# Regrouping transposed x and the attention rows R by way of HBM, in six transfers a block where there were sixteen

## The chip, the cores and the metric

The kernel runs on one core of one Trainium2 chip. The metric is the device time of one execution in microseconds (us), as the median of several runs. Differences below about 0.3% (3.4 us) cannot be told from no change in this kernel.

A core has five engines with a queue each: PE (TensorE, matmuls; its weight loads are listed as PEld), DVE (VectorE), ACT (ScalarE), POOL (GpSimd) and SP (SyncE). SP computes nothing here: it issues nearly all DMA transfers, one after the other, in the order in which the program wrote them. An instruction that waits, on any engine, holds everything written behind it on that engine.

## What is computed

Two stages over x of shape (4, 12608, 128). The first is an attention by way of 32 inducing rows, used forth and back; the second is a channel mix with a shift by one token.

```python
h = mab(I, x)                  # 32 rows attend to all 12608 tokens of a batch
x = mab(x, h)                  # each token attends to the 32 rows of h
x_prev = shift(x, 1)           # the token before, 0 for the first
xk = mu_k * x + (1 - mu_k) * x_prev
xr = mu_r * x + (1 - mu_r) * x_prev
k = maximum(xk @ w_k, 0)       # 128 -> 1024
v = k * k @ w_v                # 1024 -> 128
out = sigmoid(xr @ w_r) * v
# mab(q, kv): softmax(q @ kv.T / sqrt(128)) @ kv
```

## The kernel before, in words

**The mix sets the rhythm.** The second attention's output is never formed. Its weights R (32 rows a token, held as rounded part and remainder) go straight into matmuls with W, which is h folded into the weights of the mix. Tokens of a batch are taken in 25 groups: 24 of 512 tokens and one of 320. A group takes four *units*, so there are 100 units a batch and 400 in all, emitted by the loop `for n in range(len(units) + LAG + 2)`. In unit n, PE first runs `up` of unit n (L809, L811: W times R into PSUM), then, in a group's second unit, `zgate` (L798, L799), then `down` of unit n - 4 (L840, six matmuls). DVE squeezes the result of `up` (L821, L823), ACT squares it (L826, L827), POOL takes a difference (L829). When a group is done, DVE multiplies by the gate (L845) and transposes the result (L856, in `store`), and for every second group SP issues four output transfers (L864) of 128 KB each.

**The attention is woven in by hand.** `at(n, f)` files a step f to be emitted at the end of unit n, after that unit's `down`; `soon(n, f)` files it right behind `up` of unit n. Steps of one n keep the order in which they were filed. In the loop the output transfers of a finished group stand ahead of the steps of the same unit: the store of group g falls into unit 4g + 9, for odd g of a batch in units 13, 21, 29 and so on, counted from the first unit of that batch.

A *block* is four groups (2048 tokens); a batch has six blocks and the short rest. With t the batch's first unit (4 in the first batch) and s = t + 12 j:

- `stage_a(b + 1, j, at, s)` treats block j of the *next* batch. `btr(c)`, for c = 0..3 at s - 1, s, s + 1, s + 3, transposes a quarter of the block in 32 x 32 squares on DVE (L344) into an `xs` tile of 128 x 512. Its four 32-row strips belong to four groups, and four transfers (L347) bring each to rows 32c..32c+31 of one group's transposed x (`xt`). So a block takes 16 transfers of 64 KB. The scores (L372: eight matmuls, all reading `xt`) are filed at s + 9, and the load of the following block (L193, 1 MB) at s + 5.
- `stage_b(b, j + 1, at, s + 1)` makes R of the next block of the *running* batch: scores (L616), softmax, then `high` (ACT, L656, the rounded part `ah`) at 7 and `low` (DVE, L660, the remainder `al`) at 9 units behind its start, and `spread(i)` for i = 0..3 at 10 + i. Each spread makes one group's R tile of 128 x 513: its column 0 is the last column of the group before (`halo`, L593, a transfer of 0.5 KB), and its four 32-row quarters are ah, al, ah, al of that group (L670, four transfers of 64 KB). The first unit that reads the block j + 1 of a batch is unit 16 (j + 1) of that batch. For the first of these blocks that is 16 units into the batch, against a first spread at unit 11 of it; later blocks have ever more time, since blocks are made every 12 units and used every 16. A `quick` variant, with fewer units between its steps, serves block 1 of the first batch and block 0 of the second.
- The first block of the first batch is made in the head (`start`), by transposes on PE and copies on ACT into R (`put`, L771 and L773), with three one-column copies on DVE for column 0 (L595). The copy for group 1 (`put1`) is filed behind `up` of unit 2, and the gate's weights (`wg`) and the scores of groups 2 and 3 (`sc2`) at the end of unit 1.

Of the kernel before, what the change touches and what calls it, by code (L numbers as in the profile page):

```python
# [19 lines left out]
def kernel(  # L20
# [11 lines left out]
    nc = tc.nc  # L32
# [21 lines left out]
    st = ctx.enter_context(tc.tile_pool(name="st", bufs=1))  # L54
    wp = ctx.enter_context(tc.tile_pool(name="wp", bufs=2))
    sm = ctx.enter_context(tc.tile_pool(name="sm", bufs=2))
    r_pool = ctx.enter_context(tc.tile_pool(name="r_pool", bufs=10))
    mp = ctx.enter_context(tc.tile_pool(name="mp", bufs=2))
    pa = ctx.enter_context(tc.tile_pool(name="pa", bufs=2, space=bass.MemoryType.PSUM))
    pv = ctx.enter_context(tc.tile_pool(name="pv", bufs=2, space=bass.MemoryType.PSUM))  # L60
    pb = ctx.enter_context(tc.tile_pool(name="pb", bufs=1, space=bass.MemoryType.PSUM))
# [26 lines left out]
    def load_weight(dst, src, n, raw):  # L88


        if src.dtype == F32:
            nc.sync.dma_start(out=dst, in_=src)
            return lambda: None
        raw = raw.bitcast(I32)[:, :2 * n]
        rv = raw
        if len(src.shape) == 3:
            rv = raw.rearrange("p (c d) -> p c d", c=src.shape[1])
        nc.sync.dma_start(out=rv, in_=src.bitcast(I32))

        def steps():  # L100
            v = nc.vector
            w2 = raw.rearrange("p (n h) -> p h n", h=2)
            lo, hi = w2[:, 0, :], w2[:, 1, :]
            o = next(turns)
            t = st.tile([P, G], I32, name=("s2", "ah")[o])[:, :n]
            q = st.tile([P, G], F32, name=("e1t", "aT")[o], bufs=1)[:, :n]
            m = st.tile([P, G], I32, name="xs", bufs=4)[:, :n]
            r = st.tile([P, G], I32, name="xs", bufs=4)[:, :n]
            qv, tv = q, t.bitcast(F32)
            if len(dst.shape) == 3:  # L110
                qv = qv.rearrange("p (c d) -> p c d", d=C)
                tv = tv.rearrange("p (c d) -> p c d", d=C)
            v.tensor_scalar(out=t, in0=hi, scalar1=20, scalar2=0x7FF,
                            op0=ALU.logical_shift_right, op1=ALU.bitwise_and)
            nc.scalar.activation(out=t, in_=t, func=AF.Relu, scale=-1.0, bias=bias[0])
            nc.scalar.activation(out=t, in_=t, func=AF.Relu, scale=-2.0 ** 23, bias=bias[1])
            v.tensor_scalar(out=m, in0=hi, scalar1=0xFFFFF, scalar2=0x100000,
                            op0=ALU.bitwise_and, op1=ALU.bitwise_or)
            v.tensor_scalar(out=r, in0=hi, scalar1=-2147483648, scalar2=0x35800000,
                            op0=ALU.bitwise_and, op1=ALU.bitwise_or)  # L120
# [205 lines left out]
    def stage_a(b, j, at, t):  # L326
# [12 lines left out]
        def btr(c):  # L339
            if c == 0:  # L340
                for i in range(Q):
                    xt_tile(S, j, i)
            xs = st.tile([P, G], F32, name="xs", bufs=4)
            nc.vector.transpose(out=xs.rearrange("p (s q) -> p s q", q=M),  # L344
                                in_=S.xb[j][:, :, M * c:M * (c + 1)])
            for i in range(Q):
                nc.sync.dma_start(out=S.xt[j, i][M * c:M * (c + 1), :], in_=xs[M * i:M * (i + 1)])  # L347

        def t_tr():
            ps = pb_tile("a")  # L350
# [108 lines left out]

        for c in range(Q):  # L460
            at(t + (-1, 0, 1, 3)[c], lambda c=c: btr(c))
        if tail:
            at(t + 5, t_tr)
            soon(t + 11, t_scores)
# [21 lines left out]
    def combine(b, at=None, t=0):  # L486
# [57 lines left out]
                                        in1=dst.bitcast(F32)[P // 2:], op=ALU.subtract)  # L544
            return prod, high, low

        def wpack(parts, cw, tags, t):

            X = {}
            rows = M * len(parts)  # L550

            def prod():
                X["ps"] = pb_tile("a")
                for n, (s, nm, c0, src) in enumerate(parts):
                    nc.tensor.matmul(out=X["ps"][M * n:M * (n + 1), :cw], lhsT=L["h4"][nm][:, :M], rhs=src,
                                     start=True, stop=True)

            def high():
                X["hi"] = st.tile([P, G], F32R, name=tags[0], bufs=tags[2])[:rows, :cw]
                nc.scalar.copy(out=X["hi"], in_=X["ps"][:rows, :cw])  # L560

            def low():
                lo = st.tile([P, G], F32R, name=tags[1], bufs=tags[2])[:rows, :cw]
                hi = X["hi"].bitcast(F32)
                nc.vector.tensor_tensor(out=lo, in0=X["ps"][:rows, :cw], in1=hi, op=ALU.subtract)
                X["hl"] = (hi, lo.bitcast(F32))

            def spread(n):
                s, nm, c0, src = parts[n]
                for q in range(Q):  # L570
                    nc.sync.dma_start(out=S.W[s].bitcast(F32)[M * q:M * (q + 1), c0:c0 + cw],
                                      in_=X["hl"][q // 2][M * n:M * (n + 1)])
            at(t, prod)
            at(t, high)
            at(t + 1, low)
            for n in range(len(parts)):
                at(t + 1 + n, lambda n=n: spread(n))
# [2 lines left out]
            return weights, hfin, gates, wpart  # L580
        at(t + 9, weights)
        at(t + 10, hfin)
        parts = [(s, f"k{s}", c * G, wk_sb[:, c * G:(c + 1) * G]) for c in range(F // G) for s in range(2)]
        for n in range(0, len(parts), Q):
            wpack(parts[n:n + Q], G, ("ah", "al", 1), t + 11 + 4 * (n // Q))
        wpack([(s, f"r{s}", F, wr_sb) for s in range(2)], C, ("xs", "xs", 4), t + 13)

    def halo(S, g, far=True):

        if g == 0:  # L590
            nc.vector.memset(S.R[g].bitcast(F32)[:, 0:1], 0.0)
        elif far:
            nc.sync.dma_start(out=S.R[g].bitcast(F32)[:, 0:1], in_=S.R[g - 1].bitcast(F32)[:, G:G + 1])  # L593
        else:
            nc.vector.tensor_copy(out=S.R[g][:, 0:1], in_=S.R[g - 1].bitcast(F32)[:, G:G + 1])  # L595


    def stage_b(b, j, at, t, quick=False):
# [62 lines left out]

        def spread(i):
            src = (L["ah"].bitcast(F32), L["al"].bitcast(F32))
            if full or i == 0:
                S.R[j * Q + i] = r_pool.tile([P, G + 1], F32R, name="R")
                halo(S, j * Q + i)
            R = S.R[j * Q + (i if full else 0)].bitcast(F32)
            o, lo = (0, 0) if full else (offs[i], i * w - offs[i])
            for q in range(Q):
                nc.sync.dma_start(out=R[M * q:M * (q + 1), 1 + o + lo:1 + o + w],  # L670
                                  in_=src[q % 2][M * i:M * (i + 1), lo:w])

        if quick:
            at(t, scores)
            for n, f in ((1, trans), (1, maxi), (1, sub), (2, total), (2, recip), (3, mult), (3, back), (4, low)):
                at(t + n, f)
            soon(t + 2, expo)
            soon(t + 4, high)
            for i in range(Q):
                at(t + 5 + i, lambda i=i: spread(i))  # L680
            return
        at(t, scores)
        at(t + 1, trans)
# [6 lines left out]
        at(t + 6, back)  # L690
        at(t + 7, high)
        at(t + 9, low)
        for i in range(Q):
            at(t + 10 + i, lambda i=i: spread(i))

    def stage_b_head(gs):

# [6 lines left out]
        def part(ks):  # L704
# [4 lines left out]
            def scores():  # L709
                if ks[0] == 0:  # L710
                    L["ps"] = pb_tile("b")
                for k in ks:
# [3 lines left out]
                        nc.tensor.matmul(out=L["ps"][M * i:M * (i + 1), k * P:(k + 1) * P], lhsT=S.hT,  # L716
                                         rhs=xv[:, i], start=True, stop=True)
                    del S.xt[0, g]
                    if g not in S.R:
                        S.R[g] = r_pool.tile([P, G + 1], F32R, name="R")  # L720

            def turn():
                if ks[0] == 0:
# [197 lines left out]
    def head():  # L921
# [15 lines left out]
        for k in range(n - 2):  # L937
# [12 lines left out]
                last.hmm(h)  # L950
            nxt.scores()
            last.acc()
        S.R[0] = r_pool.tile([P, G + 1], F32R, name="R")
        halo(S, 0)
        u, v, w = bl[n - 3:]
        w.tr(1)
        v.maxi()
# [37 lines left out]
    def start():  # L995
# [15 lines left out]
        def gate_bank(s):  # L1011
            if s == 0:
# [7 lines left out]
        S = batches[0]  # L1020
        run([gates, sc0, sc1, tu0, df0, ex0, wa[0][0], wa[1][0], wb[0][0], lambda: spin(2), tu1, nm0, wa[0][1], hi0,
             wa[1][1], wb[0][1], lo0, wa[0][2], put0, lambda: spin(2),
             df1, ex1, wa[1][2], nm1, hi1, lambda: halo(S, 1, far=False)])
        for n, f in ((0, wb[1][0]), (0, wb[1][1]), (2, put1)):
            soon(n, f)
        for n, f in ((0, wb[0][2]), (0, lo1), (0, wb[1][2]), (1, sc2), (2, tu2), (2, df2), (2, ex2), (3, nm2)):
            at(n, f)
        for prod, high, low in wg:
            at(1, prod)
        for prod, high, low in wg:  # L1030
            at(1, high)
            at(2, low)
        for k, (high, low, put) in enumerate(pl1):
            at(3, high)
            at(4, low)
            soon(2 * k + 6, put)
            at(4 * k + 4, lambda k=k: halo(S, k + 2, far=False))
        soon(4, lambda: units[0][0].zgate(first=True))

    SEG = 12  # L1040
# [71 lines left out]
```

## Time and profile before

| | |
|---|---|
| runs, median (lowest to highest) | 1118.56 us (1115.95 to 1118.95), 3 runs |
| profiled execution, its own time | 1117.51 us |
| its span, first to last instruction | 1115.1 us |
| granted PE clock over the span | 0.998 |
| DVE, ACT, POOL busy | 82%, 87%, 85% of the span |
| transfers on SP's queue that regroup x | 288 of 64 KB |
| transfers that regroup R of whole blocks | 368 of 64 KB |

How to read the rows: a row of the timeline has the start in us from the span's start, the duration in us, engine, line, operation, output<-input, shapes, and xN where N like instructions were merged into one row. The time in square brackets is how long the engine sat idle ahead of it, and who ended that. A merged row of SP shows how long SP took to issue those transfers, not how long they flew; the time from issue to landing stands in the list of DMA issues. PE rows overlap: a matmul of 512 columns lasts 0.39 us, but the next begins 0.23 us after it.

### The profile page before, as it was taken

What the parts mean: (1) busy time and instruction counts of PE and PEld (TensorE: products, weight loads), DVE (VectorE), ACT (ScalarE), POOL (GpSimd) and SP (SyncE); (2) the same over time, 40 slices, a digit from 0 to 9 for tenths busy, and PEclk for the clock granted to TensorE, in tenths of its full rate; (3) what the DMA queues carried; (4) which work ended last, traced back from release to release, by engine and by line L of the source; (5) the groups of instructions that cost most, each with busy time, mean ns of one, the idle gap of its engine ahead of it and who ended that gap; (6) DMA issues with size and microseconds to landing.
All of it is one profiled execution on the core that took longest, in us unless ns stands there. A gap on an engine that the chain in (4) does not pass through costs nothing.

```text
span 1115.1 us, 17659 instructions
## 1 busy us (share of the span) xinstructions
PE 1093.0 (98%) x5707; PEld 830.1 (74%) x5707; DVE 911.3 (82%) x1317; ACT 969.8 (87%) x1097; POOL 953.0 (85%) x417
## 2 busy tenths in 40 slices
PE   7899999999999999999999999999999999999997
PEld 4577777777777777777787777777777777777886
DVE  6889889987778898986678988988676888887665
ACT  6698888898889888887988988888889999989996
POOL 3388988888898888888878998888798899999997
PEclk9999999999999999999999999999999999999999
DMA  9034555642345555464234555654222233242212
GB/s 342 11 86 93 109 128 117 136 97 64 62 84 124 125 121 122 94 127 94 36 74 90 116 122 125 133 123 94 43 53 57 51 65 59 53 74 57 44 29 34
DMA packets 264458, 102.30 MB, mean 92 GB/s; under 512 B 234256, under 2 KB 237488, under 8 KB 262064
## 3 DMA queue, kind: packets, MB, share of 16 engines
q1 hardware_dynamic: 263360, 101.10, 41.8%
q8 instruction: 45, 0.74, 0.3%
q14 instruction: 45, 0.37, 0.1%
q10 hardware_dynamic: 1008, 0.10, 0.1%
HBM read 28.07 MB, written 25.82 MB: 48 GB/s over the span
## 4 chain that ended last, share of the span: by engine, by line
PE 86%; DVE 5%; ACT 4%; DMA 3%; issue 1%; POOL 1%; SPq 0%; ACTq 0%; DVEq 0%; POOLq 0%
PE ps_v L840 44%; PE ps_a L809 16%; PE ps_a L811 15%; PE pb_b L616 2%; PE pb_a L372 2%; PE ps_v L798 2%; PE ps_v L799 2%; DVE k_t L821 2%; DMA xb<-in_x_dram 2%; PE pb_a L441 2%; ACT kh L826 1%; ACT k_t L827 1%; DMA kl<-in_x_dram 1%; POOL kl L829 1%; DMA mur<-in_moe_mu_r_dram 0%
## 5 line engine op out<-in xcount | busy, mean ns | idle before, releaser
L829 POOL TENSOR_TENSOR kl<-k_t,kh 128x1024 fp32r<-128x1024 f32 (+1 forms) x399 | 938.6, 2385 | 128.1 <-ACT k_t L827 105.0
L821 DVE TENSOR_SCALAR k_t<-ps_a 128x1024 f32<-128x1024 f32 (+1 forms) x400 | 479.8, 1200 | 142.9 <-PE ps_a L811 115.5
L827 ACT ACTIVATE k_t<-k_t 128x1024 f32<-128x1024 f32 (+1 forms) x400 | 418.4, 1048 | 34.6 <-DVE kh L823 22.4
L826 ACT ACTIVATE kh<-k_t 128x1024 fp32r<-128x1024 f32 (+1 forms) x352 | 365.8, 1039 | 81.5 <-PE ps_v L840 40.7
L809 PE MATMUL ps_a<-R,W 128*128 128x512 f32 (+1 forms) x800 | 323.5, 405 | 2.6 <-ACT R L773 1.6
L811 PE MATMUL ps_a<-R,W 128*128 128x512 f32 (+1 forms) x800 | 313.8, 392 | 0.0
L840 PE MATMUL ps_v<-kh,wvh 128*128 128x512 f32 (+1 forms) x800 | 248.0, 391 | 0.0
L840 PE MATMUL ps_v<-kl,wvh 128*128 128x512 f32 (+1 forms) x800 | 246.8, 390 | 0.8
L840 PE MATMUL ps_v<-kh,wvl 128*128 128x512 f32 (+1 forms) x800 | 247.0, 390 | 0.0
L809 PEld LDWEIGHTS ps_a<-R,W 128*128 128x128 f32 x800 | 150.7, 188 | 76.1 <-issue 12.2
L840 PEld LDWEIGHTS ps_v<-kl,wvh 128*128 128x128 f32 x800 | 148.4, 188 | 38.0 <-POOL kl L829 6.0
L840 PEld LDWEIGHTS ps_v<-kh,wvh 128*128 128x128 f32 x800 | 149.3, 188 | 34.6
L840 PEld LDWEIGHTS ps_v<-kh,wvl 128*128 128x128 f32 x800 | 149.6, 188 | 33.8
L811 PEld LDWEIGHTS ps_a<-R,W 128*128 128x128 f32 x800 | 150.4, 188 | 30.4 <-issue 0.2
L845 DVE TENSOR_TENSOR oT<-ps_v,rT 128x512 f32<-128x512 f32 (+1 forms) x100 | 66.7, 667 | 1.8
L856 DVE STREAM_TRANSPOSE ot<-oT 128x512 f32<-128x512 f32 x96 | 67.2, 700 | 0.0
L823 DVE SCALAR_TENSOR_TENSOR kh<-ps_a,k_t 128x1024 fp32r<-128x1024 f32 x48 | 58.8, 1225 | 5.1
L801 ACT ACTIVATE rT<-ps_v 128x512 f32<-128x512 f32 (+1 forms) x99 | 57.9, 585 | 0.3
L344 DVE STREAM_TRANSPOSE xs<-xb 128x512 f32<-128x512 f32 x72 | 50.0, 694 | 4.9 <-DMA xb<-in_x_dram 4.3
L798 PE MATMUL ps_v<-R,W 128*128 128x512 f32 (+1 forms) x99 | 39.1, 395 | 1.6 <-DVE oT L845 1.6
L801 ACT ACT_TABLE_LOAD x31 | 39.8, 1283 | 0.5
L799 PE MATMUL ps_v<-R,W 128*128 128x512 f32 (+1 forms) x99 | 38.7, 391 | 0.0
(215 smaller groups left out, 611.4 us busy)
## 6 DMA issues: line engine op xcount, KB each, us to landing
out_dram<-ot SPq DMA_DIRECT2D x184, 128.0 KB, 3.3
xb<-in_x_dram SPq DMA_DIRECT2D x18, 1024.0 KB, 5.7
xt<-xs SPq DMA_DIRECT2D x288, 64.0 KB, 2.0
R<-ah SPq DMA_DIRECT2D x184, 64.0 KB, 2.0
R<-al SPq DMA_DIRECT2D x184, 64.0 KB, 2.0
kl<-in_x_dram SPq DMA_DIRECT2D x4, 512.0 KB, 9.8
xb<-in_x_dram SPq DMA_DIRECT2D x4, 512.0 KB, 11.0
W<-ah SPq DMA_DIRECT2D x24, 64.0 KB, 2.0
```

Source lines behind the costliest of these rows:

```text
L798: nc.tensor.matmul(out=ps[:, :w], lhsT=S.W[0][:, F:WF], rhs=R[:, 1:w + 1], start=True, stop=False)
L799: nc.tensor.matmul(out=ps[:, :w], lhsT=S.W[1][:, F:WF], rhs=R[:, 0:w], start=False, stop=True)
L801: nc.scalar.activation(out=self.rT, in_=ps[:, :w], func=AF.Sigmoid)
L809: nc.tensor.matmul(out=ps[:, c, :w], lhsT=S.W[0][:, cs], rhs=R[:, 1:w + 1], start=True, stop=False)
L811: nc.tensor.matmul(out=ps[:, c, :w], lhsT=S.W[1][:, cs], rhs=R[:, 0:w], start=False, stop=True)
L821: nc.vector.tensor_scalar(out=k, in0=self.ps[:, :, :w], scalar1=0.0, scalar2=None, op0=ALU.max)
L826: nc.scalar.activation(out=kh, in_=k, func=AF.Square)
L827: nc.scalar.activation(out=k, in_=k, func=AF.Square)
L829: return lambda eng, a, z: eng.tensor_tensor(out=kl[:, :, a:z], in0=k[:, :, a:z], in1=kh.bitcast(F32)[:, :, a:z], op=ALU.subtract)
L840: nc.tensor.matmul(out=self.v, lhsT=wt[:, fc, :], rhs=kk[:, c, :], start=(fc == 0 and n == 0), stop=(fc == FC - 1 and n == 2))
L845: nc.vector.tensor_tensor(out=self.oT, in0=self.v, in1=self.rT, op=ALU.mult)
L856: nc.vector.transpose(out=ot[:, o:o + w], in_=self.oT)
```

## The change

Both regroupings go through scratch tiles in HBM (`dr`, two of each kind).

- **x**: two quarters share one `xs` tile of 128 x 1024; behind quarters 1 and 3 it is written to HBM in one transfer (512 KB). A new step `regroup(c)` reads rows 32c..32c+31 of all four groups back into the block's `xt` in one transfer (256 KB). They are filed at s + 2, s + 2, s + 5, s + 5.
- **R**: `ah` and `al` are each written to HBM by one transfer (256 KB, `send`), and four transfers of 256 KB (`fetch`) read them back, each filling 32 rows of all four groups. R of a block is one tile of 128 x 2049 (`rows`), so only its first column needs a transfer; the columns in between are shared by neighbouring groups. The short rest of a batch keeps its old transfers. `send(0)` is filed one unit ahead of `low` (with it in the quick variant), `send(1)` one unit after; fetches 0 and 2 two units after, fetches 1 and 3 three units after.
- **Head**: `put1` moves from behind `up` of unit 2 to behind `up` of unit 1, and with it, from the end of unit 1, `sc2` and the gate's weights' matmuls and casts. The one-column copies go.

```diff
-    r_pool = ctx.enter_context(tc.tile_pool(name="r_pool", bufs=10))
+    r_pool = ctx.enter_context(tc.tile_pool(name="r_pool", bufs=3))
+    dr = ctx.enter_context(tc.tile_pool(name="dr", bufs=2, space=bass.MemoryType.DRAM))
...
-            xs = st.tile([P, G], F32, name="xs", bufs=4)
+                L["d"] = dr.tile([2, P, 2, G], F32, name="xd")
+            if c % 2 == 0:
+                L["xs"] = st.tile([P, 2 * G], F32, name="xs", bufs=2)
+            xs = L["xs"][:, c % 2 * G:(c % 2 + 1) * G]
             nc.vector.transpose(out=xs.rearrange("p (s q) -> p s q", q=M),
                                 in_=S.xb[j][:, :, M * c:M * (c + 1)])
-            for i in range(Q):
-                nc.sync.dma_start(out=S.xt[j, i][M * c:M * (c + 1), :], in_=xs[M * i:M * (i + 1)])
+            if c % 2:
+                nc.sync.dma_start(out=L["d"][c // 2].rearrange("p c g -> p (c g)"), in_=L["xs"])
+
+        def regroup(c):
+            nc.sync.dma_start(out=S.xtb[j][M * c:M * (c + 1)],
+                              in_=L["d"][c // 2, :, c % 2, :].rearrange("(i m) g -> m i g", i=Q))
...
             at(t + (-1, 0, 1, 3)[c], lambda c=c: btr(c))
+            at(t + (2, 2, 5, 5)[c], lambda c=c: regroup(c))
...
+    def rows(S, j):
+
+        t = S.Rb = r_pool.tile([P, Q * G + 1], F32R, name="R")
+        for i in range(Q if j < NBLK - 1 else 1):
+            S.R[j * Q + i] = t[:, i * G:(i + 1) * G + 1]
+        first = S.R[j * Q].bitcast(F32)[:, 0:1]
+        if j == 0:
+            nc.vector.memset(first, 0.0)
         else:
-            nc.vector.tensor_copy(out=S.R[g][:, 0:1], in_=S.R[g - 1].bitcast(F32)[:, G:G + 1])
+            nc.sync.dma_start(out=first, in_=S.R[j * Q - 1].bitcast(F32)[:, G:G + 1])
...
+        def send(q):
+            if q == 0:
+                L["d"] = dr.tile([2, P, G], F32, name="rd")
+            nc.sync.dma_start(out=L["d"][q], in_=L["ah" if q == 0 else "al"].bitcast(F32))
+
+        def fetch(q):
+            if q == 0:
+                rows(S, j)
+            nc.sync.dma_start(out=S.Rb.bitcast(F32)[M * q:M * (q + 1), 1:].rearrange("m (i g) -> m i g", i=Q),
+                              in_=L["d"][q % 2].rearrange("(i m) g -> m i g", i=Q))
+
+        def placed(n):
+            if not full:
+                for i in range(Q):
+                    at(n + 1 + i, lambda i=i: spread(i))
+                return
+            at(n if quick else n - 1, lambda: send(0))
+            at(n + 1, lambda: send(1))
+            at(n + 2, lambda: fetch(0))
+            at(n + 2, lambda: fetch(2))
+            at(n + 3, lambda: fetch(1))
+            at(n + 3, lambda: fetch(3))
...
-            for i in range(Q):
-                at(t + 5 + i, lambda i=i: spread(i))
+            placed(t + 4)
...
-        for i in range(Q):
-            at(t + 10 + i, lambda i=i: spread(i))
+        placed(t + 9)
...
-             df1, ex1, wa[1][2], nm1, hi1, lambda: halo(S, 1, far=False)])
-        for n, f in ((0, wb[1][0]), (0, wb[1][1]), (2, put1)):
+             df1, ex1, wa[1][2], nm1, hi1])
+        for n, f in ((0, wb[1][0]), (0, wb[1][1]), (1, put1), (1, sc2)):
             soon(n, f)
-        for n, f in ((0, wb[0][2]), (0, lo1), (0, wb[1][2]), (1, sc2), (2, tu2), (2, df2), (2, ex2), (3, nm2)):
+        for n, f in ((0, wb[0][2]), (0, lo1), (0, wb[1][2]), (2, tu2), (2, df2), (2, ex2), (3, nm2)):
             at(n, f)
         for prod, high, low in wg:
-            at(1, prod)
+            soon(1, prod)
         for prod, high, low in wg:
-            at(1, high)
+            soon(1, high)
             at(2, low)
...
-            at(4 * k + 4, lambda k=k: halo(S, k + 2, far=False))
```

More of the change, by code (lines that the diff above doesn't have):

```diff
@@ L106, in steps @@
             q = st.tile([P, G], F32, name=("e1t", "aT")[o], bufs=1)[:, :n]
-            m = st.tile([P, G], I32, name="xs", bufs=4)[:, :n]
-            r = st.tile([P, G], I32, name="xs", bufs=4)[:, :n]
+            mr = st.tile([P, 2 * G], I32, name="xs", bufs=2)
+            m, r = mr[:, :n], mr[:, G:G + n]
             qv, tv = q, t.bitcast(F32)
@@ L545, in wpart, with wpack @@
             return prod, high, low
-        def wpack(parts, cw, tags, t):
+        def wpack(parts, cw, tiles, t):
             X = {}
@@ L558, in high @@
             def high():
-                X["hi"] = st.tile([P, G], F32R, name=tags[0], bufs=tags[2])[:rows, :cw]
+                X["hi"], X["lo"] = (t[:rows, :cw] for t in tiles())
                 nc.scalar.copy(out=X["hi"], in_=X["ps"][:rows, :cw])
             def low():
-                lo = st.tile([P, G], F32R, name=tags[1], bufs=tags[2])[:rows, :cw]
+                lo = X["lo"]
                 hi = X["hi"].bitcast(F32)
@@ L582, in combine, with pair, one_tile @@
         at(t + 10, hfin)
+        def pair():
+            return [st.tile([P, G], F32R, name=nm) for nm in ("ah", "al")]
+        def one_tile():
+            t = st.tile([P, 2 * G], F32R, name="xs", bufs=2)
+            return t[:, :G], t[:, G:]
         parts = [(s, f"k{s}", c * G, wk_sb[:, c * G:(c + 1) * G]) for c in range(F // G) for s in range(2)]
         for n in range(0, len(parts), Q):
[L585 to L593, printed above, removed]
+            wpack(parts[n:n + Q], G, pair, t + 11 + 4 * (n // Q))
+        wpack([(s, f"r{s}", F, wr_sb) for s in range(2)], C, one_tile, t + 13)
+    def rows(S, j):
[5 more added lines that the diff above has]
+            nc.vector.memset(first, 0.0)
         else:
-            nc.vector.tensor_copy(out=S.R[g][:, 0:1], in_=S.R[g - 1].bitcast(F32)[:, G:G + 1])
+            nc.sync.dma_start(out=first, in_=S.R[j * Q - 1].bitcast(F32)[:, G:G + 1])
     def stage_b(b, j, at, t, quick=False):
@@ L663, in spread @@
             src = (L["ah"].bitcast(F32), L["al"].bitcast(F32))
-            if full or i == 0:
-                S.R[j * Q + i] = r_pool.tile([P, G + 1], F32R, name="R")
-                halo(S, j * Q + i)
+            if i == 0:
+                rows(S, j)
             R = S.R[j * Q + (i if full else 0)].bitcast(F32)
@@ L671, in spread @@
                                   in_=src[q % 2][M * i:M * (i + 1), lo:w])
+        def send(q):
[4 more added lines that the diff above has]
+            if q == 0:
+                rows(S, j)
+            nc.sync.dma_start(out=S.Rb.bitcast(F32)[M * q:M * (q + 1), 1:].rearrange("m (i g) -> m i g", i=Q),
[11 more added lines that the diff above has]
+            at(n + 3, lambda: fetch(3))
         if quick:
@@ L718, in scores @@
                     del S.xt[0, g]
-                    if g not in S.R:
-                        S.R[g] = r_pool.tile([P, G + 1], F32R, name="R")
             def turn():
@@ L952, in head @@
             last.acc()
-        S.R[0] = r_pool.tile([P, G + 1], F32R, name="R")
-        halo(S, 0)
+        rows(S, 0)
         u, v, w = bl[n - 3:]
```

## The prediction

> **What bounds the kernel now.** First the page: the span, and each engine's share of it.
>
> ```profile
> span 1115.1 us, 17659 instructions
> PE 1093.0 (98%) x5707; PEld 830.1 (74%) x5707; DVE 911.3 (82%) x1317; ACT 969.8 (87%) x1097; POOL 953.0 (85%) x417
> ```
>
> PE is the bound, so a change that touches only transfers gains what PE waits for transfers, and loses what new waits it makes. I looked for PE's waits next, unit by unit, in the timeline. Only two kinds depend on SP's queue. The scores of the next batch's block (L372) read `xt`; undisturbed, the eight matmuls last 1.06 us:
>
> ```profile
> 84.05 1.06 PE L372 MATMUL pb_a<-xt,indT 128*32 128x512 f32 x8
> ...
> 215.68 1.83 PE L372 MATMUL pb_a<-xt,indT 128*32 128x512 f32 x8
> ...
> 375.60 2.00 PE L372 MATMUL pb_a<-xt,indT 128*32 128x512 f32 x8
> ...
> 442.10 1.46 PE L372 MATMUL pb_a<-xt,indT 128*32 128x512 f32 x8
> ...
> 509.80 2.62 PE L372 MATMUL pb_a<-xt,indT 128*32 128x512 f32 x8 [0.32 <-PE ps_v L840]
> ...
> 647.10 1.68 PE L372 MATMUL pb_a<-xt,indT 128*32 128x512 f32 x8
> ...
> 778.66 2.18 PE L372 MATMUL pb_a<-xt,indT 128*32 128x512 f32 x8
> ```
>
> Of the 18 such sets seven are stretched (the one at 149.7 stands in the chain of waits in pieces): at 149.7, 215.7, 375.6, 442.1, 509.8, 647.1 and 778.7 us, by 0.4, 0.8, 0.9, 0.4, 1.9 (the idle time ahead of it included), 0.6 and 1.1 us. Sum: 6.1 us. The reason is that SP runs behind:
>
> ```profile
> 492.86 0.70 DVE L344 STREAM_TRANSPOSE xs<-xb 128x512 f32<-128x512 f32 x1
> ```
>
> ```profile
> 507.50 2.43 SPq L347 DMA_DIRECT2D xt<-xs  x4
> ```
>
> The quarter was transposed at 493.6 us and SP reached its transfers at 507.5, 13.9 us later, at 0.61 us each. The second kind is one load of the next block, issued late for the same reason, which stops DVE (2.33 us) and through it PE:
>
> ```profile
> 484.43 0.71 DVE L344 STREAM_TRANSPOSE xs<-xb 128x512 f32<-128x512 f32 x1 [2.33 <-DMA xb<-in_x_dram]
> ...
> 485.77 0.50 PE L798 MATMUL ps_v<-R,W 128*128 128x512 f32 x1 [1.27 <-DVE oT L845]
> ```
>
> That is 1.3 us, so **7.4 us** is all that PE now loses to SP's queue.
>
> **What goes and what comes on SP.** The list of DMA issues:
>
> ```profile
> out_dram<-ot SPq DMA_DIRECT2D x184, 128.0 KB, 3.3
> xb<-in_x_dram SPq DMA_DIRECT2D x18, 1024.0 KB, 5.7
> xt<-xs SPq DMA_DIRECT2D x288, 64.0 KB, 2.0
> R<-ah SPq DMA_DIRECT2D x184, 64.0 KB, 2.0
> R<-al SPq DMA_DIRECT2D x184, 64.0 KB, 2.0
> ...
> R<-R SPq DMA_DIRECT2D x93, 0.5 KB, 1.7
> ...
> kh<-in_x_dram SPq DMA_DIRECT2D x4, 256.0 KB, 4.4
> ```
>
> There go 288 + 368 + 93 = 749 transfers. There come 18 blocks of six, 23 of six, and one first column for each of 24 blocks after a batch's first: 108 + 138 + 24 = 270. At 0.61 us an issue SP is relieved of some 290 us. By itself that is worth nothing (SP computes nothing); its worth is the 7.4 us above. I take that in full if the longer route of x is on time. Its price: a write of 512 KB, then reads of 256 KB. The trace has neither; between its 64 KB row (2.0 us) and its 1024 KB row (5.7 us) a straight line gives 3.9 us per MB: 2.7 us for 256 KB, 3.7 for 512 KB. Quarter 3's transposes end at 493.6 in the case above; a write issued then lands at 497.3, the reads are filed two units later (4.7 us, 498.3), and two of them, 512 KB together, land at about 502; the scores were due at 509.5. Some seven us are left, and some three to four where an output store (about 3 us of issuing) stands ahead of the reads. So x is in time.
>
> **What R's longer route costs.** This is the term on which the sign hangs. Fetches 1 and 3 are filed three units behind `low`, where the first spread was filed one unit behind it, and they bring rows that *all* groups of the block need. For blocks made early against their use this changes nothing. The first block of a batch's count that stage_b makes (the one for unit 16) has three units left from there, and in unit 13 of the batch, where its fetches 1 and 3 are filed, the loop first emits an output store, which waits for DVE's transposes. SP takes the three in order: store, fetch 1, fetch 3. So I read for each such place when the transposes (L856) end, how long the four stores took to issue, and when `up` (L809) first reads the block:
>
> ```profile
> 84.95 0.70 DVE L856 STREAM_TRANSPOSE ot<-oT 128x512 f32<-128x512 f32 x1
> ...
> 127.44 0.69 DVE L856 STREAM_TRANSPOSE ot<-oT 128x512 f32<-128x512 f32 x1
> ...
> 353.69 0.69 DVE L856 STREAM_TRANSPOSE ot<-oT 128x512 f32<-128x512 f32 x1
> ...
> 624.93 0.69 DVE L856 STREAM_TRANSPOSE ot<-oT 128x512 f32<-128x512 f32 x1
> ...
> 891.82 0.70 DVE L856 STREAM_TRANSPOSE ot<-oT 128x512 f32<-128x512 f32 x1
> ```
>
> ```profile
> 86.30 3.07 SPq L864 DMA_DIRECT2D out_dram<-ot  x4
> ...
> 892.55 2.69 SPq L864 DMA_DIRECT2D out_dram<-ot  x4
> ```
>
> ```profile
> 89.77 0.40 PE L809 MATMUL ps_a<-R,W 128*128 128x512 f32 x1
> ...
> 133.58 0.40 PE L809 MATMUL ps_a<-R,W 128*128 128x512 f32 x1
> ...
> 359.43 0.40 PE L809 MATMUL ps_a<-R,W 128*128 128x512 f32 x1
> ...
> 631.02 0.40 PE L809 MATMUL ps_a<-R,W 128*128 128x512 f32 x1
> ...
> 897.52 0.40 PE L809 MATMUL ps_a<-R,W 128*128 128x512 f32 x1
> ```
>
> The places are units 16, 32 (the first batch counts four units later), 116, 216 and 316. From the end of the transposes to the use there are 4.1, 5.4, 5.0, 5.4 and 5.0 us. In them must fit 0.1 us to start, the store's issue (3.1, three times 3.0, 2.7), and the pair of fetches. The pair, 512 KB, lands 3.7 us after the first issue by the line above. I add 0.6 for the stores still moving ahead of it: the last store's 3.3 us runs 1.3 past a small transfer's 2.0, and the fetch is issued 0.7 behind it. So 4.3 for the pair, and R is late by 3.4, 2.0, 2.4, 2.0 and 2.1 us: **11.9 us**. PE has nothing else to do there, since `up` stands first in its unit. Bounds for the pair: 2.6 us, if each lands like a 64 KB transfer, the second 0.6 behind; 5.7 + 0.6 us, if the pair is as slow as the 1024 KB load. That makes 1.7 less or 2.0 more at each place: 3.4 to 21.9 us. I take the middle, which lies on the line through both rows; the 256 KB row of 4.4 us is from the initial burst of loads and stands for the upper part.
>
> [...]
>
> New waits on SP (reads that wait for writes) hold the stores and loads behind them, each for at most one write's flight. Before, SP was up to 13.9 us late; the 290 us freed cover this, and nobody waits for a store early.
>
> **The head.** `up` of unit 4, group 1's first, waits 1.40 us for the copy of R:
>
> ```profile
> 55.25 0.50 PE L809 MATMUL ps_a<-R,W 128*128 128x512 f32 x1 [1.40 <-ACT R L773]
> ```
>
> ```profile
> 52.24 1.06 ACT L826 ACTIVATE kh<-k_t 128x1024 fp32r<-128x1024 f32 x1 [0.94 <-DVE k_t L821]
> ...
> 54.30 0.41 ACT L540 CAST W<-ps_v 128x128 fp32r<-128x128 f32 x2
> 54.60 0.60 ACT L773 CAST R<-pb_a 128x512 fp32r<-128x512 f32 x1
> ...
> 61.45 0.60 ACT L801 ACTIVATE rT<-pb_a 128x512 f32<-128x512 f32 x1
> ```
>
> The copy (0.60) and the casts (0.41) move into ACT's 0.94 us of idle time, so unit 4 starts up to 1.4 us earlier. But PE then meets the gate's activation, which ends at 62.05: the transposes for group 2 start right behind it, at 62.10. That activation stands behind DVE's chain (L821 of units 2 to 4, the softmax of groups 2 and 3). This chain starts later rather than earlier, because `up` of unit 2 now waits for four transposes. So the gain is given back within three units. I take 0; the ends are a gain of 1.4 us and a loss of about 0.6, a copy's length.
>
> **The sum**, against the profiled execution's own time (span 1115.1, execution 1117.5): -7.4 + 11.9 + 0 = +4.5, so **1122.0 us**. The median shown is 1118.6, 1.0 above that execution; runs of before differ by 3 us, so I leave the sum where it is.
>
> **The rivals.**
>
> *The fetches land soon.* Faster, the other side: at the lower bound the late R costs 3.4 us, the relief stays at 7.4, and with up to 1.4 from the head the time is 1112 to 1113.5. It turns at a landing of 3.4 us for the pair, where both terms are equal. For it: 64 KB transfers issued 0.6 us apart kept landing in 2.0, so the engines had room. Against it: even then unit 16 has 4.1 us for 3.2 of store and 2.6 of flight. [...] Chance 0.2.
>
> *The terms cancel*, with a landing of 3 to 3.6 us: 1115.5 to 1118.5, chance 0.15.
>
> *The removed transfers did not hold the scores.* Then the change does not do what it is for, the relief is 0, and the late R alone makes 1129.4. For it: the waits view puts part of these waits down to PE's own L840. Against it: SP's 13.9 us. Chance 0.05.
>
> *The HBM route is slow everywhere*, landings like the 1024 KB row: R costs 21.9 us and in blocks with a store ahead of the reads x has little left, 1132. Chance 0.1.
>
> **How the numbers follow.** My forecast, +1 to +9 around 1122, has 0.5; about 0.2 of it lies below +3.4 us, the 0.3% that a measurement of this kernel can tell from no change. Faster: 0.2. Same: 0.15 + 0.2 = 0.35. Slower: 0.3 + 0.05 + 0.1 = 0.45. The likeliest case's own range is 1118.5 to 1126.5; the range over the cases runs from 1110.5, the soon-landing rival with something to spare, to 1130, short of the slowest.
>
> **What would show it.** In the profile of after: the score sets (L372) all last about 1.06 us, and SP's regroupings start within 2 us of being due; else the first term is wrong. At units 16, 32, 116, 216 and 316 `up` stands idle 2 to 3.4 us for a transfer into R, issued behind a store; if it doesn't, or the pair lands in under 3 us, the second is wrong, and the kernel is faster. PE's waits at other first units of blocks, or on `xt`, would mean slower transfers than I priced.

## The result, and the profile after

| | before | after |
|---|---|---|
| median of the runs (lowest to highest), us | 1117.30 (1115.95 to 1118.95) | 1147.63 (1147.58 to 1148.92) |
| profiled execution, its own time, us | 1117.51 | 1147.67 |
| its span, us | 1115.1 | 1145.4 |
| granted PE clock over the span | 0.998 | 0.987 |

The changed kernel is slower: ratio 1.0285, 95% interval 1.0268 to 1.0302. The forecast was 1122.0 with a range from 1110.5 to 1130, so the sign was right and the size was not: the time lies 15 us above even the slowest rival (1132).

From the page of the changed kernel, the span and the engines' shares:

```profile
span 1145.4 us, 16778 instructions
...
PE 1105.5 (97%) x5707; PEld 837.7 (73%) x5707; DVE 912.3 (80%) x1314; ACT 970.7 (85%) x1097; POOL 953.2 (83%) x417
```

Two things stand there. PE is busy 12.5 us longer with the same 5707 matmuls, which goes with the lower granted clock (0.987 for 0.998), and the span grew by 30.3 us, so that PE is idle 17.8 us longer. The page's list of DMA issues gives the landings that the prediction had to estimate:

```profile
R<-rd SPq DMA_DIRECT2D x92, 256.0 KB, 4.0
...
xb<-in_x_dram SPq DMA_DIRECT2D x18, 1024.0 KB, 7.3
xd<-xs SPq DMA_DIRECT2D x36, 512.0 KB, 3.0
xt<-xd SPq DMA_DIRECT2D x72, 256.0 KB, 4.6
rd<-ah SPq DMA_DIRECT2D x23, 256.0 KB, 3.4
rd<-al SPq DMA_DIRECT2D x23, 256.0 KB, 2.4
```

A read of 256 KB into 32 rows takes 4.0 to 4.6 us, longer than a write of 512 KB from 128 rows (3.0). No line through sizes alone gives that. Next the idle time of PE, from the groups by line: before the change the score matmuls (L372) and the first matmul of `up` (L809), then the same two after it (now L380 and L846).

```profile
L372 PE MATMUL pb_a<-xt,indT 128*32 128x512 f32 x144 | 25.0, 604 | 0.3 <-PE ps_v L840 0.3
L809 PE MATMUL ps_a<-R,W 128*128 128x512 f32 (+1 forms) x800 | 323.5, 405 | 2.6 <-ACT R L773 1.6
```

```profile
L846 PE MATMUL ps_a<-R,W 128*128 128x512 f32 (+1 forms) x800 | 326.1, 408 | 20.9 <-DMA R<-rd 8.7 <-issue 7.8 <-DMA xt<-xd 2.7
L380 PE MATMUL pb_a<-xt,indT 128*32 128x512 f32 x144 | 19.2, 604 | 0.8 <-DMA xt<-xd 0.4 <-PE ps_v L877 0.4
```

The score sets are no longer stretched (25.0 to 19.2 us, by 5.8), and they stand idle only 0.8 us in all, of which the row puts 0.4 down to x. But `up` now sits idle for 20.9 us where it sat 2.6. These are the waits of over 0.5 us, from the timeline of PE, in the order of units 16, 32, 100, 116, 216 and 316:

```profile
95.41 0.47 PE L846 MATMUL ps_a<-R,W 128*128 128x512 f32 x1 [3.89 <-issue]
...
145.48 0.77 PE L846 MATMUL ps_a<-R,W 128*128 128x512 f32 x1 [4.32 <-DMA R<-rd]
...
334.46 0.47 PE L846 MATMUL ps_a<-R,W 128*128 128x512 f32 x1 [1.69 <-DMA R<-rd]
...
380.23 0.47 PE L846 MATMUL ps_a<-R,W 128*128 128x512 f32 x1 [2.65 <-DMA R<-rd]
...
651.44 0.46 PE L846 MATMUL ps_a<-R,W 128*128 128x512 f32 x1 [2.73 <-DMA xt<-xd]
...
923.67 0.77 PE L846 MATMUL ps_a<-R,W 128*128 128x512 f32 x1 [3.86 <-issue]
```

Together 19.1 us, at the five predicted places (17.4 us) and at unit 100, which the prediction left out. Three rows name something other than R as what ended the wait ("issue", `xt`). SP's timeline shows what it was; at unit 16 and at unit 316:

```profile
87.19 2.67 SPq L901 DMA_DIRECT2D out_dram<-ot  x4
89.91 1.61 SPq L699 DMA_DIRECT2D R<-rd  x2
```

```profile
914.61 3.51 SPq L901 DMA_DIRECT2D out_dram<-ot  x4
918.16 1.76 SPq L699 DMA_DIRECT2D R<-rd  x2
```

At unit 16 the second fetch was issued at 90.8 and took some 4.4 us from issue to landing, so it landed at about 95.3, where the wait ends. At unit 216, where the row names `xt`, the two fetches were there by 651.2 and `up` began at 651.44; x's first read, issued at 647.5, landed only after 4.8 us, at 652.3. From the issue of the first to the use it is 5.5 us at unit 16 (89.91 to 95.41) and at unit 316 (918.16 to 923.67). At unit 32 the pair was issued at 138.13, right behind another store, and used at 145.48: 7.3 us. Each fetch of that pair took 6.0 us by itself.

What follows each wait is the second half of the loss. The table by stretch, for the 3.8 us behind each of the six waits: busy time and count of PE, PEld, DVE, ACT and POOL, then the granted PE clock, DMA share and GB/s.

```profile
95.40:99.20 3.80, 3.79 (x10) 2.97 (x11) 1.84 (x2) 0.60 (x1) 1.41 (x1) 0.60 0.00 0
145.40:149.20 3.80, 3.72 (x9) 2.98 (x10) 1.23 (x1) 0.35 (x2) 0.55 (x1) 0.50 0.26 94
334.40:338.20 3.80, 3.74 (x12) 3.35 (x13) 1.85 (x2) 1.12 (x2) 3.65 (x3) 0.59 0.00 0
380.20:384.00 3.80, 3.77 (x16) 3.12 (x17) 2.40 (x3) 1.77 (x3) 3.35 (x2) 1.00 0.65 184
651.40:655.20 3.80, 3.76 (x11) 3.05 (x12) 2.12 (x2) 1.71 (x3) 3.25 (x2) 0.65 0.49 164
923.60:927.40 3.80, 3.73 (x9) 2.99 (x10) 1.23 (x1) 0.00 (x0) 3.18 (x2) 0.50 0.00 0
```

PE is busy all the while and does little: at a clock of 0.50 (97.50 to 98.55 us) a pair of `down` matmuls lasts 1.05 us where it lasted 0.63 before the wait:

```profile
90.89 0.63 PE L877 MATMUL ps_v<-kl,wvh 128*128 128x512 f32 x2
...
97.50 1.05 PE L877 MATMUL ps_v<-kh,wvl 128*128 128x512 f32 x2
```

Five of the six waits are followed by a clock of 0.50 to 0.65. What is lacking to full speed adds up to 3.8 x (0.40 + 0.50 + 0.41 + 0 + 0.35 + 0.50) = 8.2 us. In the 2 us behind each of these stretches the clock is 0.91, 0.61, 0.93, 1.00, 0.82 and 0.60, which adds 2.3 us; another 2 us on, at units 32, 216 and 316, it is 1.00 again. The account of the 30 us, by how far DVE's squeeze of each unit stands behind its place before: 1.5 us ahead of the first unit, 29.2 us around the six places (5.8, 6.6, 3.4, 2.6, 4.2 and 6.6), and -0.9 us over everything else. Of the 29.2, 19.1 is idle time. The other 10.1 is about what the slow clock makes (8.2 + 2.3 = 10.5).

### The profile page after: what moved, and what is told of

It reads as the page before. It is cut to its first block, busy times and chain, and to the rows that moved or that the text cites. A ratio compares the mean times of both kernels' runs of the same rounds, so it can differ in the third digit from the quotient of the medians.

```text
span 1145.4 us, 16778 instructions
## 1 busy us (share of the span) xinstructions
PE 1105.5 (97%) x5707; PEld 837.7 (73%) x5707; DVE 912.3 (80%) x1314; ACT 970.7 (85%) x1097; POOL 953.2 (83%) x417
## 4 chain that ended last, share of the span: by engine, by line
PE 73%; DVE 10%; ACT 6%; DMA 4%; issue 4%; SPq 2%; POOL 1%; DVEq 0%; ACTq 0%; POOLq 0%
PE ps_v L877 37%; PE ps_a L846 14%; PE ps_a L848 13%; DVE k_t L858 4%; ACT kh L863 3%; DMA R<-rd 2%; PE pb_b L635 2%; PE ps_v L835 2%; PE ps_v L836 2%; PE pb_a L449 2%; PE pb_a L380 1%; SPq L901 1%; ACT k_t L864 1%; DMA xt<-xd 1%; DVE oT L882 1%
## 5 line engine op out<-in xcount | busy, mean ns | idle before, releaser
L846 PE MATMUL ps_a<-R,W 128*128 128x512 f32 (+1 forms) x800 | 326.1, 408 | 20.9 <-DMA R<-rd 8.7
L877 PE MATMUL ps_v<-kl,wvh 128*128 128x512 f32 (+1 forms) x800 | 252.0, 396 | 0.4
L877 PE MATMUL ps_v<-kh,wvh 128*128 128x512 f32 (+1 forms) x800 | 250.8, 395 | 0.0
L877 PE MATMUL ps_v<-kh,wvl 128*128 128x512 f32 (+1 forms) x800 | 250.8, 395 | 0.0
L846 PEld LDWEIGHTS ps_a<-R,W 128*128 128x128 f32 x800 | 152.3, 190 | 99.0 <-issue 31.2
L848 PEld LDWEIGHTS ps_a<-R,W 128*128 128x128 f32 x800 | 151.9, 190 | 31.4 <-issue 0.2
```

Source lines behind the costliest of these rows:

```text
L846: nc.tensor.matmul(out=ps[:, c, :w], lhsT=S.W[0][:, cs], rhs=R[:, 1:w + 1], start=True, stop=False)
L848: nc.tensor.matmul(out=ps[:, c, :w], lhsT=S.W[1][:, cs], rhs=R[:, 0:w], start=False, stop=True)
L877: nc.tensor.matmul(out=self.v, lhsT=wt[:, fc, :], rhs=kk[:, c, :], start=(fc == 0 and n == 0), stop=(fc == FC - 1 and n == 2))
```

## The experiments

**Theory.** Fetches 1 and 3 stand in SP's order behind an output store, in a unit three ahead of their use, and so are late; the rest of the loss is the PE clock, which is low after such a wait (0.50 to 0.65 after five of the six above). **Rivals:** the longer route of x; the transfers by HBM being slow wherever they stand; the head.

### The parts alone

x_only takes the new route for x and leaves R with 16 transfers and the head as before.

```diff
# from the changed kernel: send, fetch, placed and rows go, as does the moved head
-        placed(t + 9)
+        for i in range(Q):
+            at(t + 10 + i, lambda i=i: spread(i))
```

> Only x is regrouped by way of HBM; R keeps its sixteen transfers a block, and the head is as before. Theory 'late R' (all of the loss is R landing after its block's first unit, and the slow PE clock behind each such wait; x's relief of SP's queue is real): 1110 us, 7 us under before, the stretched score sets back at 1.06 us. Rival 'traffic' (the detour by HBM slows things wherever it is used): no gain, 1117 us or more.

Measured: 1150.07 us (1146.59 to 1155.46), ratio 1.0308 (1.0283 to 1.0333). My theory that the late R is all fell here: x alone is as slow as both together. It is a figure that the recorded rival would give (1117 or more), so that rival stands until the runs below. The waits of PE:

```profile
PE pb_a L380 <- DMA xt<-xd: 26.6, 12, 3.2
```

Sixteen of the 18 score sets stand idle, 32.4 us together: the row's twelve, and four whose idle time is put down to other things. One of them, from the timelines of DVE, SP and PE:

```profile
205.92 0.70 DVE L348 STREAM_TRANSPOSE xs<-xb 128x512 f32<-128x512 f32 x1
```

```profile
211.47 1.82 SPq L686 DMA_DIRECT2D R<-ah  x1
213.33 0.59 SPq L686 DMA_DIRECT2D R<-al  x1
213.97 1.08 SPq L354 DMA_DIRECT2D xt<-xd  x2
215.09 0.43 SPq L351 DMA_DIRECT2D xd<-xs  x1
219.89 0.96 SPq L354 DMA_DIRECT2D xt<-xd  x2
```

```profile
225.10 1.50 PE L380 MATMUL pb_a<-xt,indT 128*32 128x512 f32 x8 [3.22 <-DMA xt<-xd]
```

The quarter was ready at 206.6; SP, busy with R's many small transfers, issued its write at 215.1, the reads could only go at 219.9, and the scores came at 225.1. A lag of SP that cost the old single hop 0.8 us (the set at 215.7 in the prediction) costs the double hop 3.2.

r_only takes the new route for R and the moved head, and leaves x with its 16 transfers.

```diff
# from the changed kernel: the write to HBM and regroup go
-            at(t + (2, 2, 5, 5)[c], lambda c=c: regroup(c))
...
+            for i in range(Q):
+                nc.sync.dma_start(out=S.xt[j, i][M * c:M * (c + 1), :], in_=xs[M * i:M * (i + 1)])
```

> Only R goes by way of HBM, with the moved head; x keeps its sixteen transfers a block, so SP's queue stays behind. Theory 'late R': the loss of the change without its relief, 1146 us or more; since SP is late again, the fetches can only be later: 1146 to 1160. Rival 'traffic': half of the added bytes, so about half of the loss, 1130 us.

Measured: 1153.64 us (1149.39 to 1155.73), ratio 1.0336 (1.0309 to 1.0363). That is within the theory's range. The waits of `up` at the six places are together longer than in the full change, 26.1 us against 19.1, the longest 6.1. SP also has x's 16 transfers a block to issue here; at unit 316, in the last batch, where no next batch's x is regrouped, the wait is 2.8 and not longer than before (3.9). The row lists one short wait more, and leaves out one that is put down to `xt`:

```profile
PE ps_a L831 <- DMA R<-rd: 22.7, 6, 6.1
```

So the two halves don't add: +34 us for x, +38 for R, +30 to 31 for both. Each half lightens SP, and by these waits that is what the other's longer route needs; the next run tests it for x, no run does for R.

head_only is the kernel before with the moved head alone.

```diff
-        for n, f in ((0, wb[1][0]), (0, wb[1][1]), (2, put1)):
+        for n, f in ((0, wb[1][0]), (0, wb[1][1]), (1, put1), (1, sc2)):
...
```

> The kernel before with the moved head alone: group 1's transposes and copy, the scores of groups 2 and 3 and the gate's weights behind the matmuls of unit 1; no other part of the change. In the changed kernel the squeeze of unit 2 came 0.6 us later and that of unit 7 took back 0.4: 1116.2 us, no change that can be told. If instead the wait of 1.4 us that went is kept: 1114.6 us. The first unit, which came 1.4 us later in all kernels with a scratch tile in HBM, should start where it did before.

Measured: 1116.76 us, ratio 1.0000 (0.9988 to 1.0011). The head is worth nothing that can be told, either way.

### Is x_only slow because SP is late?

x_few_stores is x_only with one of the four output transfers of a store in the first three batches, so that part of the output isn't written.

```diff
-                for i in range(Q):
+                for i in range(Q if g == NG - 1 or self.b == B - 1 else 1):
```

> x alone by way of HBM, and in the first three batches one output transfer of each store's four instead of all, so that part of the output is left out: SP gets some 120 transfers or 85 us less to issue. The run with x alone was slow (1150 us); the theory 'late R' fell there. New theory 'late SP': with R's sixteen transfers still on SP's queue, which runs up to 14 us behind, x's write and then its reads are each late. By that the waits at the score sets (32 us and the clock) shrink to a third or less: 1120 to 1128 us. Rival 'long route': the write and the reads take too long by themselves; then they stay: 1145 us or more.

Measured: 1111.08 us (1110.43 to 1111.99), ratio 0.9957 (0.9942 to 0.9972); that is 39 us less than x_only, for 108 issues of SP fewer. That is below what the theory gave (1120 to 1128). The wait for x is gone:

```profile
PE pb_a L380 <- DMA xt<-xd: 0.6, 2, 0.4
```

The run also writes less output to HBM, but less traffic is not what x needed: the changed kernel moves more than x_only, 133 MB against 121, and its score sets hardly wait. Issues and output stores ahead of the reads on SP are not told apart by this run.

before_few_stores makes the same edit in the kernel before, to tell what a prompt SP is worth there.

> The kernel before, with one output transfer of each store's four in the first three batches, so that part of the output is left out. SP has some 85 us less to issue and nothing else changes. If all that PE loses to SP's lag in the kernel before is what the prediction read off (7.4 us in the profiled execution, less in others): 1110 to 1112 us, as with x by HBM and few stores (1111.1 us). If x's HBM route is worth something by itself, this stays 3 us or more above that run.

Measured: 1110.11 us (1109.07 to 1110.72), ratio 0.9954 (0.9940 to 0.9967), or 5.1 us. Its score sets last as long as in the changed kernel:

```profile
L372 PE MATMUL pb_a<-xt,indT 128*32 128x512 f32 x144 | 19.2, 605 | 0.0
```

So the prompt SP is worth 5.1 us (3.7 to 6.7) where 7.4 was predicted, and given that, x by HBM adds nothing that can be told (0.9957 against 0.9954).

### Is R late because of its place?

fetch_early files fetches 1 and 3 one unit earlier, in the unit ahead of the store.

```diff
-            at(n + 3, lambda: fetch(1))
-            at(n + 3, lambda: fetch(3))
+            at(n + 2, lambda: fetch(1))
+            at(n + 2, lambda: fetch(3))
```

> The change, with fetches 1 and 3 filed with fetches 0 and 2, one unit earlier, so that at units 16, 32, 116, 216 and 316 they stand ahead of the output store. Theory 'late R': these five waits go, the one at unit 100 stays (3.4 us with its slow clock), the relief of 7 us shows: 1113 to 1115 us. Rival 'flight' (the reads take too long whatever stands ahead of them): waits of 1 to 2 us stay at each place, 1125 us or more.

Measured: 1117.97 us (1116.43 to 1120.62), ratio 1.0025 (1.0013 to 1.0037). That is 3 us more than the theory gave (1113 to 1115): the late R went, but the relief of 7 us does not show. SP now issues all four fetches ahead of the store, and of the six waits only that at unit 100 is left:

```profile
82.50 1.95 SPq L699 DMA_DIRECT2D R<-rd  x4
87.07 3.26 SPq L901 DMA_DIRECT2D out_dram<-ot  x4
```

```profile
PE ps_a L846 <- DMA R<-rd: 1.6, 1, 1.6
```

Nearly the whole loss goes with one unit. The transfers are the same ones, so they are not slow "wherever they stand".

store_behind leaves the fetches in their unit and lets the store of just that unit come after them.

```diff
+            behind = n in (13, 29, 113, 213, 313)
...
-                units[m - 1][0].store()
+            if due and not behind: units[m - 1][0].store()
             old.down(ou)
             run(events.pop(n, []))
+            if due and behind: units[m - 1][0].store()
```

> The change, with one order turned round: in units 13, 29, 113, 213 and 313 the steps filed for the unit, the fetches 1 and 3 among them, are emitted ahead of the output store instead of behind it. Nothing is filed earlier. If the order behind the store is what made R late: the pair is issued some 4 to 5 us earlier and the waits at units 16, 32, 116, 216 and 316 go or shrink below 1 us, with them most of the slow clock: 1117 to 1123 us. If one unit less of time is what counted (that fetches 1 and 3 stand in the third unit): waits of 2 us and more stay, 1135 us or more.

Measured: 1119.35 us (1117.42 to 1120.97), ratio 1.0028 (1.0016 to 1.0040). The store's transposes on DVE are emitted later with it, and the unit's `down` and other steps also come before it; otherwise nothing is changed. Five turns in the emitted order bring back 28 us. What is left is unit 100:

```profile
PE ps_a L846 <- DMA R<-rd: 2.0, 1, 2.0
```

al_direct keeps slot and store, but brings the rows of q = 1 and 3 from `al` directly, in eight transfers of 64 KB, group by group. It asks how much of the delay is the slot and how much is what stands in it.

```diff
-            at(n + 1, lambda: send(1))
...
-            at(n + 3, lambda: fetch(1))
-            at(n + 3, lambda: fetch(3))
+            for i in range(Q):
+                at(n + 3, lambda i=i: direct(i))
```

> The changed kernel, in which rows of q = 1 and 3 come without HBM: at the same step, n+3, and behind the same output store, eight transfers of 64 KB take them from al to R, group by group, in place of the one write and the two fetches. Theory (the slot behind the store makes the data late, and the size of the fetch adds to it, since group 0 waits for rows of all four groups): group 0's two small transfers are the first behind the store and land in about 2.0 us instead of 5.5 to 7.3 for the pair. The idle time of PE before units 16, 32, 116, 216 and 316 falls from 17.4 us together to 3 to 7 us, little of the slow clock after it stays, unit 100 keeps 1 to 2 us: 1117 to 1123 us. Rival (the slot behind the store alone decides, whatever is fetched there): the waits keep most of their length, 1138 us or more. Second rival (eight transfers instead of three make SP late for x's reads): new waits of PE at the score sets, L380, over 1130 us.

Measured: 1123.65 us (1121.15 to 1124.67), ratio 1.0064 (1.0045 to 1.0084), just above what the theory gave and far below its first rival. At unit 16 the idle time is 1.58 us instead of 3.89, and no slow matmuls follow:

```profile
93.00 0.47 PE L850 MATMUL ps_a<-R,W 128*128 128x512 f32 x1 [1.58 <-DMA R<-al]
...
94.02 0.63 PE L881 MATMUL ps_v<-kh,wvh 128*128 128x512 f32 x2
```

The five waits are 1.58, 0.69, 0.31, 0.27 and 0.87: 3.7 us in place of 17.4. So of the slot's 17.4 us only 3.7 remain when small transfers stand in it, the first group's first. The slot and what is fetched there make the delay together. The edit changes two things about that, the size and the route (no HBM and no write to wait for), and which of them counts is not told apart. At unit 100, which was to keep 1 to 2 us, `up` no longer waits. Part of what keeps the time above 1117 is four score sets that wait, 4.6 us together, as the second rival has it, but mixed (below) has such waits too, 2.9 us, without the eight transfers; so that these are to blame is not shown. One of them:

```profile
121.72 1.06 PE L380 MATMUL pb_a<-xt,indT 128*32 128x512 f32 x8 [1.42 <-DVE ot L897]
```

### How much is the slow clock?

fill puts matmuls whose result is overwritten ahead of `up` at the six places, so that PE is not idle in the wait.

```diff
+            fill = {16: 22, 32: 22, 100: 10, 116: 14, 216: 14, 316: 22}.get(self.b * UB + self.g * NU + u, 0)
+            for i in range(fill):
+                nc.tensor.matmul(out=ps[:, 0, :P], lhsT=ident, rhs=ident, start=True, stop=True)
```

> The change, with 22, 22, 10, 14, 14 and 22 matmuls of 128 x 128 on constants ahead of the first matmul of units 16, 32, 100, 116, 216 and 316, to be overwritten: they fill the wait for R, which itself stays. If the slow units behind each wait come from PE's clock falling while it is idle, they go, and 9 to 10 us with them: 1138 us, granted clock back at 1.00 there. If they have another cause (data still landing, other engines behind), the time stays at 1147 us, or rises by what the added matmuls overrun.

Measured: 1140.19 us (1138.89 to 1142.01), ratio 1.0222 (1.0199 to 1.0244); 7.4 us less than the changed kernel, by doing more work (9 to 10 less were expected). The fillers last 24.2 us, 5.1 more than the waits that they cover, so the gain is less than the clock's whole part. Here is the granted clock in fill behind the fillers of units 16 and 32, where the changed kernel had 0.60 and 0.50 (columns as above):

```profile
96.40:100.20 3.80, 3.80 (x18) 3.03 (x17) 2.31 (x3) 1.46 (x2) 0.35 (x1) 1.00 0.04 14
145.80:149.60 3.80, 3.80 (x17) 3.03 (x17) 2.67 (x3) 0.12 (x1) 0.00 (x0) 1.00 0.42 105
```

The clock stays at 1.00 behind all six, over the span at 0.998 instead of 0.987. So most of what the late R costs beyond the idle time is the clock.

### A version without the losses

mixed is fetch_early with the old 16 transfers of R for the first block of each batch, for unit 100 and its like.

```diff
-            if not full:
+            if not full or j == 0:
```

> The change with fetches 1 and 3 filed with 0 and 2, and in addition the first block of each batch (units 100, 200, 300) regrouped by the old sixteen transfers, each group due when its own group starts. The waits left there in the run before (1.7, 0.5 and 0.5 us, more with the clock) go: 2.5 us under the run with early fetches, which puts it 0.5 us under the kernel before: 1115.5 us. If the early blocks were not what is left, it stays 2 us over.

Measured: 1116.44 us (1115.62 to 1118.62), ratio 1.0000 (0.9991 to 1.0009). All waits of `up` for R are gone. Three score sets wait instead (0.8, 0.8 and 1.2 us), each where x's last two reads stand behind an output store; from SP's and PE's timelines:

```profile
107.59 3.54 SPq L901 DMA_DIRECT2D out_dram<-ot  x4
111.17 1.12 SPq L354 DMA_DIRECT2D xt<-xd  x2
```

```profile
118.43 1.06 PE L380 MATMUL pb_a<-xt,indT 128*32 128x512 f32 x8 [0.81 <-DMA xt<-xd]
```

mixed_x4 also files x's last two reads one unit earlier.

```diff
-            at(t + (2, 2, 5, 5)[c], lambda c=c: regroup(c))
+            at(t + (2, 2, 4, 4)[c], lambda c=c: regroup(c))
```

> The run called mixed, with x's last two reads filed one unit earlier (s + 4 instead of s + 5). In mixed the score sets waited at units 25, 157 and 233, where these reads stood behind an output store and landed 7 us after their issue; the squeeze came 0.9, 1.0 and 1.3 us later there. Theory 'behind the store': these waits go too, 3.2 us: 1113.3 us, under the kernel before. If the reads only wait longer for their own write, which then holds SP: no change, 1116.4 us.

Measured: 1114.15 us (1113.26 to 1115.98), ratio 0.9991 (0.9982 to 1.0000). The three waits are gone. It is the best complete kernel of the study: 1 us below the kernel before, at the edge of what can be told apart.

## Why the prediction was wrong in size

Measured against the profiled execution before, the forecast was +4.5 and the change made it +30.2. The step that failed is the price of the late R: 11.9 us in the sum, 29.2 measured around the six places. The larger part of that miss, 10.1 us, is a cost that the sum put at nothing: after five of the six waits PE's clock is low (0.50 to 0.65). The waits themselves were 5.5 too short, and one place was not looked for (1.7). A second term failed too, the relief of 7.4 us, of which 0.9 shows. Step by step:

**R late behind the store: right in mechanism and place, its waits mis-sized.** At the five units PE sits idle, for a transfer issued behind a store, as stated. Predicted were 3.4, 2.0, 2.4, 2.0 and 2.1 us, 11.9 in all; they are 3.89, 4.32, 2.65, 2.73 and 3.86, or 17.4. The prediction put the pair's landing at 4.3 us on a straight line between the 64 KB and the 1024 KB rows; it landed after 5.5 to 7.3, at unit 32 later than the upper bound given for the pair (6.3). That alone would be 8.0 us in all; the rest of the sum gave 2.5 back, chiefly because `up` came due 0.2 to 0.8 us later behind the store's transposes than in the trace of before. The 256 KB row of the first loads (4.4 us), set aside as coming from a burst, came nearer: 4.0 is the median of a single fetch, and the second of a pair is issued 0.8 behind the first. This miss is 5.5 us in all, and the sum lay within its bounds (3.4 to 21.9); by itself it would have made the time 1127.5.

**"PE has nothing else to do there", and nothing more: the omitted cost.** The prediction charged an idle microsecond as one microsecond. The trace of the changed kernel shows PE at a clock of 0.50 to 0.65 in the 3.8 us behind five of the six waits. What hangs on the waits beyond the idle time is 10.1 us; the granted clock accounts for about all of it (8.2 in these 3.8 us and 2.3 in the two behind), and fill, which keeps the clock at 1.00, got 7.4 back. The length of the wait alone doesn't tell which waits lower the clock: the three of 3.9 to 4.3 us (units 16, 32 and 316) were followed by 0.50 to 0.60, but 1.69 us at unit 100 by 0.59 and 2.73 us at unit 216 by 0.65, while unit 116 (2.65 us) kept 1.00. No run shows what decides it, and why unit 116 was spared is open.

**Unit 100: a place not looked for.** The search went through first blocks due 16 units into a batch, not through the first block of the next batch, although the kernel's description ahead of the prediction names its quick variant. From SP's timeline:

```profile
321.14 2.53 SPq L901 DMA_DIRECT2D out_dram<-ot  x4
323.77 1.22 SPq L694 DMA_DIRECT2D rd<-ah  x1
325.09 0.55 SPq L694 DMA_DIRECT2D rd<-al  x1
327.72 1.74 SPq L699 DMA_DIRECT2D R<-rd  x4
```

Store, write, write and reads one after the other: 1.69 us idle, 3.4 with what follows.

**Relief of SP, -7.4: the waits went, the time did not.** The stretched sets are all gone (5.8 of 6.1 us). Yet outside the six places the kernel is only 0.9 us ahead in this trace. Behind the load that no longer stops DVE, for one, 1.3 of 2.4 us came back within three units. Removed by itself, SP's lag is worth 5.1 us (before_few_stores). In the traces, the gains of before_few_stores are mostly in the changed kernel too (units 150 to 179: 3.1 us against 3.6), but small losses elsewhere eat them: in the last batch, from unit 330 on, PE is busy throughout at a clock of 1.00 and still falls 0.9 us behind, some 0.06 in every four units. What causes that, and where the rest went, is open.

**x in time: right, but only together with R.** The score sets stand idle 0.8 us in the changed kernel, 32.4 in x_only. The margin of 7 us was worked out for a prompt SP, which is what R's fewer transfers provide. The 3 to 4 us that were to be left behind a store are not there: in mixed such reads were late by 0.8 to 1.2.

**The head, 0: right** (1.0000 for head_only). The first unit of the changed kernel did start 1.5 us late in its trace; variants with the same head start 0.0 to 1.5 us late. It is not the head: x_only, with the head of before, starts 1.3 late, and head_only starts on time. The cause is open.

The sum of the misses: 5.5 (the five waits) + 1.7 (unit 100) + 10.1 (clock) + 6.5 (relief) + 1.5 (start) + 0.4 at the end = 25.7, the distance from +4.5 to +30.2. The rival that came nearest, HBM slow everywhere at 1132, had the size of R's idle time nearly right and the reason wrong: the same transfers one unit earlier cost next to nothing.

## What to carry to other kernels

Joining the transfers of several consumers into one gives all of them the deadline of the first, so before counting issues saved, find the tightest use and see what stands ahead of the transfer on its in-order queue; here one unit, or one turn with a store, was worth some 28 us, and a prompt SP, which 479 fewer issues were to bring, about 5 (before_few_stores). Don't price a wait of the engine that sets the time at its length alone (here 19.1 us of waits cost 29.2, though 2.65 at unit 116 cost 2.6), but from traces in which it waited and the clock is shown. And take the latency of a transfer from a row of like shape and direction, not from a line through sizes (here the line gave 2.7 us for a read of 256 KB; the row of the first loads had 4.4, and the reads took 4.0 to 4.6).

## What the runs showed of the hardware

- Of three waits of 1.7 to 2.7 us, two (units 100 and 216) were followed by a PE clock of 0.59 and 0.65 and one (unit 116) by 1.00; keeping PE busy with idle matmuls in the wait made the kernel 7.4 us faster.
- By its medians a 256 KB read from HBM into 32 rows took 4.0 to 4.6 us in the changed kernel, a write of the same size from 128 rows 2.4 to 3.4 and one of 512 KB 3.0. Two such reads behind a store, with x's reads behind them, took 6.0 each (unit 32).
- The page's releaser can be off: two of the six waits were put down to "issue" and one to `xt`, though by the landings it was R that arrived at their end.
